# Seeding PSUM banks from ScalarE and VectorE in a seven-product matmul scheme, with a new order of the products

## The chip, the cores and the metric

The kernel runs on one core of one Trainium2 chip. The metric is device time in microseconds, the median of the runs; lower is better.

## The reference

```python
x = A_x                                   # (1, 1, 8192, 448)
xn = _layernorm(x, axis=-1)
s = _A_ref(xn, ...)                       # spectral mixer: rfft2, two block-diagonal
                                          # complex layers (4 blocks of 112), soft threshold, irfft2
g = _silu(_B_ref(xn, w_gate, w_up, w_down))
                                          # (gelu(x @ w_gate) * (x @ w_up)) @ w_down, 448 -> 1792 -> 448
return x + s * g
```

Everything is fp32. 8192 tokens go through both branches.

## The kernel before

**Precision.** Each fp32 factor is split into a high and a low fp16 part; a product of two such factors is three matmuls (high·high, low·high, high·low) that accumulate in fp32 in PSUM.

**Stages.** The FFN branch is the bulk of the work on TensorE. Its 1792 hidden columns are worked in two passes: pass p = 0 takes 8 blocks of 128 columns, pass p = 1 takes 6 (`PF`, L30). In each pass the 8192 tokens go by in 16 chunks (`NG`) of 512 tokens. The first two chunks of pass 0 are done plainly (`plain`). All others, 14 chunks of pass 0 and 16 of pass 1, use a seven-product (Strassen-Winograd) scheme over 2x2 blocks: two hidden blocks, gate and up, and two token halves. Beside the FFN run, in this order, the normalisation and forward transform (beside pass 0), the spectral groups (beside pass 1), and the inverse transform with the final gating (beside the end of pass 1).

**A unit** (`unit`, L1026) is one pair of hidden blocks of one chunk: 4 units in a chunk of pass 0, 3 in a chunk of pass 1, 104 in all. It has seven products, 1, 5, 6, 7, 2, 3 and 4 (`PROD`, `product`, L985). Products 1, 5, 6 and 7 are 12 matmuls of 256 columns, products 2, 3 and 4 are 10. Each goes into a PSUM bank of 512 fp32 columns; `start=True` on the first matmul of a group begins a sum afresh, later ones accumulate.

There are four rings of two PSUM banks each: `BX`, `BY`, `BD`, `BF` (L404). In a unit:

- X (a BX bank) takes product 1, then 6, 7 and 4 on top. ACT copies X after product 1 to `p1` (ring U1, trace name u) and after product 6 to `v1` (ring V1, trace name v); DVE adds `p5` to X after product 7 and writes `v2` (ring V2, trace name v).
- Y (a BY bank) takes product 5, which ACT copies to `p5` (ring U5, trace name u), then product 3 on top.
- Z (a BY bank) takes product 2 alone.
- `c11` on DVE adds Z to `p1`, then ACT takes the gelu of that. `c12` adds Y to `v1` on DVE, then `glu` (L1010, a scalar_tensor_tensor) multiplies gelu, scale and that sum: the hidden values of token half 0. `c21` takes the gelu of X after product 4, and `glu` multiplies it with `v2`: half 1.
- The hidden values are split to fp16 (`h`): ACT casts, DVE or POOL subtracts. In pass 1 `sums` makes the sums that the down projection's own seven-product scheme needs, in pieces of a weight tile (trace name wt).

**Order on TensorE.** `chunk` (L1442) emits, unit after unit, products 1, 5, then product 4 of the unit before, then 6, 2, 3, 7; in the last unit of a chunk of pass 1 it is 2, 7, 3. After the last unit come its product 4 and the down projection (`down` in pass 0, `down2` in pass 1, trace tiles bd). In pass 1 the last part of `down2`, called `tail`, is kept back and run in the next chunk after its first unit's product 5. Vector work after the down projection adds into `pt`.

**What sets the order of everything else.** The program is emitted by a planner (`Pace`, L49). Tasks are generators; each instruction is issued at a planned time that follows from the planner's own costs and from when the operands are ready, and the order of issue is the order in that engine's queue. The engines then run their queues in order and wait on semaphores. Rings (`Ring`, L221) hand out buffers and PSUM banks; a task that finds none free waits until one is put back. All engine calls go through one helper, so every row of the profile has its line, L199, and rows are told apart by their tiles.

Of the kernel before, what the change touches and what calls it, by code (L numbers as in the profile page):

```python
# [11 lines left out]
F32 = mybir.dt.float32  # L12
I32 = mybir.dt.int32
AF = mybir.ActivationFunctionType
ALU = mybir.AluOpType
# [6 lines left out]
NG = 16  # L22
# [351 lines left out]
def afno_geglu_kernel(ctx, tc, x, gu, wd, mlp, b1, b2, c_m, c_mt, c_small, out):  # L374
# [22 lines left out]
    def ring(pool, shape, dt, name, bufs):  # L397
        return Ring(pace, pool, shape, dt, name, bufs)
# [84 lines left out]
    XTB = ring(fp, [128, (XW - XA) // 128, 256], F16, "xtb", 1)  # L483
    HT = ring(fp, [128, PF[0][1], 2, 512], F16, "h", 1)
    U1 = ring(fp, [128, 512], F32, "u1", 2)
    U5 = ring(fp, [128, 512], F32, "u5", 1)
    V1 = ring(fp, [128, 512], F32, "v1", 1)
    V2 = ring(fp, [128, 512], F32, "v2", 2)
    GL = ring(fp, [128, 512], F32, "gl", 1)
    TH = ring(fp, [128, D], F32, "th", 3)  # L490
# [534 lines left out]

    def unit(p, i, f0, h, xa):  # L1026

        m = {}

        def copy_of(R, name, bank_, at):  # L1030
            def go():
                t = m[name] = yield from R.get()
                S.copy(t, bank_)
                pace.set(m["e" + name])
            m["e" + name] = Event()
            return pace.spawn(go(), at)

        def a1():
            for e in range(2):
                yield ev("comb", f0 + e) if p == 0 else ev("far", f0 + e)  # L1040
            m["X"] = yield from BX.get()
            product(1, m["X"], xa, f0, True, False)
            copy_of(U1, "p1", m["X"], pace.last)

        def a5():
            m["Y"] = yield from BY.get()
            product(5, m["Y"], xa, f0, True, False)
            copy_of(U5, "p5", m["Y"], pace.last)

        def a6():  # L1050
            yield m["ep1"]
            product(6, m["X"], xa, f0, False, False)
            copy_of(V1, "v1", m["X"], pace.last)

        def a2():
            m["Z"] = yield from BY.get()
            product(2, m["Z"], EV["xtb", p, i], f0, True, True)
            m["c11"] = pace.spawn(c11(), pace.last)

        def c11():  # L1060
            u = m["p1"]
            V.tensor_tensor(u, m["Z"], u, op=ALU.add)
            BY.put(m["Z"])
            yield
            gelu(p, f0, u, u)
            yield

        def a3():
            yield m["ep5"]
            product(3, m["Y"], EV["xtb", p, i], f0, False, True)  # L1070
            pace.spawn(c12(), pace.last)

        def c12():
            yield m["ev1"]
            v = m["v1"]
            V.tensor_tensor(v, m["Y"], v, op=ALU.add)
            BY.put(m["Y"])
            yield
            yield m["c11"]
            if p == 1:  # L1080
                g0 = m["g0"] = yield from G0.get()

                def back():
                    V1.put(v)
                    U1.put(m["p1"])

                yield from glu(p, f0, m["p1"], v, 0, h, back, g0)
                done("h", p, i, f0, 0)
                return
            yield from glu(p, f0, m["p1"], v, 0, h, lambda: V1.put(v))  # L1090
            U1.put(m["p1"])
            done("h", p, i, f0, 0)

        def a7():
            yield m["ev1"]
            product(7, m["X"], xa, f0, False, False)
            m["ec22"], m["ev2"] = Event(), Event()
            pace.spawn(c22(), pace.last)

        def c22():  # L1100
            m["v2"] = yield from V2.get()
            V.tensor_tensor(m["v2"], m["X"], m["p5"], op=ALU.add)
            pace.set(m["ev2"])
            U5.put(m["p5"])
            yield
            pace.set(m["ec22"])

        def a4():
            yield m["ev2"]
            product(4, m["X"], EV["xtb", p, i], f0, False, True)  # L1110
            pace.spawn(c21(), pace.last)

        def c21():
            gl = yield from (GL if p == 0 else GL2).get()
            gelu(p, f0, gl, m["X"])
            BX.put(m["X"])
            yield
            yield m["ec22"]
            yield from glu(p, f0, gl, m["v2"], 1, h, lambda: V2.put(m["v2"]))
            if p == 1:  # L1120
                yield from sums(gl)
                return
            GL.put(gl)
            done("h", p, i, f0, 1)

        def sums(gl):


            yield ev("h", p, i, f0, 0)
            g0, x = m["g0"], gl[:, 512:768]  # L1130
# [24 lines left out]

    def plain(c, f):

# [284 lines left out]
    def chunk(p, i):  # L1442
# [14 lines left out]
        if p == 1:  # L1457
            pace.spawn(pt_loads(i))
            if state["direct"] <= i:
                pace.spawn(load_gate(i), pace.now + 10.0)  # L1460
        prev = None
        for u in range(nf // 2):
            six, last = unit(p, i, 2 * u, h, xa)
            for n, s in enumerate(six):
                if (u, n) == (0, 2) and "tail" in state:
                    yield from state.pop("tail")()
                if (u, n) == (0, 3):
                    yield ev("xt", "b", p, i)
                if n == 2 and prev:
                    yield from prev()  # L1470
                    if (p, i) == (0, NG - 1):
                        pace.spawn(far_pair(u - 1))
                    yield pe()
# [642 lines left out]
```

## Time and profile before

| what | value |
|---|---|
| median of 3 runs | 1813.92 us (1813.49 to 1814.45) |
| profiled execution, first to last instruction | 1811.1 us |
| instructions | 39096 |
| TensorE matmuls | 15709 |
| VectorE busy | 1395.7 us, 2497 instructions |
| ScalarE busy | 1059.9 us, 2015 instructions |
| GpSimd busy | 470.3 us, 550 instructions |
| HBM | 124 GB/s over the span |

The profile is of one execution, with busy time per engine; times in it are microseconds, means of one instruction nanoseconds. In a row, `out<-in` are the program's names, and a bracket at the end gives the idle time of the engine just before it and who ended it. Matmuls are pipelined and their ends are modelled.

### The profile page before, as it was taken

The page shows a single profiled execution, that of the slowest core. Times are in us where ns is not written, and L with a number is a line of the kernel's source. Part 1 is how long each engine was busy: PE and PEld are TensorE (multiplying, and loading weights), DVE is VectorE, ACT ScalarE, POOL GpSimd, SP SyncE. Part 2 cuts the span into 40 slices and gives each one's busy share as a digit, 9 for nine tenths or more (in the row PEclk, how much of TensorE's full clock was granted, in tenths as well). Part 3 has the DMA queues.
Part 4 walks back from the last instruction along what each step waited for, and adds up shares of the span by engine and source line. Part 5 has one row for each costly group of instructions (what it writes and reads, how often), then busy time and mean ns, then how long its engine had stood idle before and what let it go on. Part 6 is the DMA issues. An engine that isn't in the chain of part 4 may idle for free. (4 is left out here: it accounts for less than half of the span.)

```text
span 1811.1 us, 39096 instructions
## 1 busy us (share of the span) xinstructions
PE 1769.5 (98%) x15709; PEld 1429.6 (79%) x15709; DVE 1395.7 (77%) x2497; ACT 1059.9 (59%) x2015; POOL 470.3 (26%) x550
## 2 busy tenths in 40 slices
PE   7999999999999999999999999999999999999997
PEld 3447777767687777787887999999999998888886
DVE  7867888777865656656766888889888887888876
ACT  5746555645555444556676777777777674333343
POOL 3333432432221122100110322233223222232331
PEclk9999999999999999999999999999999999999999
DMA  6554776468655433322335624444335438999971
GB/s 217 159 151 125 201 202 193 148 196 233 168 131 162 135 111 94 94 66 75 88 126 155 163 83 119 119 109 92 94 104 119 114 80 222 296 303 304 291 234 44
DMA packets 345733, 277.03 MB, mean 153 GB/s; under 512 B 231536, under 2 KB 316784, under 8 KB 345552
## 3 DMA queue, kind: packets, MB, share of 16 engines
q1 hardware_dynamic: 345264, 273.98, 53.5%
q8 instruction: 123, 2.02, 0.5%
q10 hardware_dynamic: 288, 0.56, 0.1%
q14 instruction: 58, 0.48, 0.1%
HBM read 123.31 MB, written 102.02 MB: 124 GB/s over the span
## 5 line engine op out<-in xcount | busy, mean ns | idle before, releaser
L199 PEld LDWEIGHTS <-wt 128*128 128x128 f16 x9350 | 909.7, 98 | 173.3 <-issue 17.8
L199 PE MATMUL bx<-xta,wt 128*128 128x256 f16 (+1 forms) x3843 | 473.6, 275 | 0.3 <-ACT v L199 0.2
L199 PEld LDWEIGHTS <-h 128*128 128x128 f16 x2688 | 257.1, 98 | 131.8 <-DVE h L199 4.5
L199 PE MATMUL bd<-dw,h 128*128 128x448 f16 (+1 forms) x1920 | 345.5, 329 | 3.4 <-DVE h L199 2.8
L199 PE MATMUL by<-xtb,wt 128*128 128x256 f16 x2080 | 251.2, 272 | 0.0
L199 PE MATMUL by<-xta,wt 128*128 128x256 f16 (+1 forms) x1347 | 177.0, 281 | 4.1 <-DVE xta L199 3.1
L199 POOL TENSOR_TENSOR wt<-wt 128x256 f32<-128x256 f32 x90 | 72.1, 801 | 304.4 <-DVE wt L199 288.0
L199 PE MATMUL bx<-xtb,wt 128*128 128x256 f16 x1040 | 130.5, 272 | 1.8 <-DVE v L199 0.9
L199 DVE TENSOR_TENSOR u<-by,u 128x512 f32<-128x512 f32 x104 | 71.5, 688 | 57.3 <-PE by L199 55.7
L199 ACT COPY u<-bx 128x512 f32<-128x512 f32 x104 | 60.9, 585 | 74.4 <-PE bx L199 73.3
L199 ACT ACTIVATE u<-u,fc 128x512 f32<-128x512 f32 (+1 forms) x118 | 77.6, 668 | 41.9 <-DVE u L199 41.9
L199 PE MATMUL bd<-dw,wt 128*128 128x224 f16 (+1 forms) x816 | 96.0, 264 | 4.7 <-DVE pt L199 4.5
L199 ACT COPY v<-bx 128x512 f32<-128x512 f32 x104 | 60.8, 585 | 63.9 <-PE bx L199 63.4
L199 ACT CAST h<-wt 128x512 f16<-128x512 f32 (+1 forms) x128 | 68.8, 538 | 47.3 <-DVE wt L199 37.4
L199 DVE SCALAR_TENSOR_TENSOR pt<-bd,fb,pt 128x448 f32<-128x448 f32 x96 | 63.5, 680 | 39.1 <-PE bd L199 38.9
L199 ACT COPY u<-by 128x512 f32<-128x512 f32 x104 | 61.0, 587 | 52.5 <-PE by L199 48.6
L199 ACT ACTIVATE th<-bd,fb 128x448 f32<-128x448 f32 x62 | 39.1, 632 | 83.5 <-PE bd L199 71.6
L199 PE MATMUL bf<-w2t,wn 112*128 112x112 f16 x1512 | 84.9, 213 | 0.0
L199 DVE SCALAR_TENSOR_TENSOR gl<-v,fc,gl 128x512 f32<-128x512 f32 (+1 forms) x70 | 47.8, 699 | 45.6 <-ACT gl L199 45.4
L199 PEld LDWEIGHTS <-wn 112*128 112x128 f16 x1512 | 80.6, 98 | 2.4
L199 DVE TENSOR_TENSOR v<-by,v 128x512 f32<-128x512 f32 x104 | 71.0, 683 | 6.4 <-PE by L199 5.8
L199 PEld LDWEIGHTS <-w1t 112*112 112x112 f16 x612 | 68.6, 130 | 7.9 <-issue 3.3
(218 smaller groups left out, 3037.7 us busy)
## 6 DMA issues: line engine op xcount, KB each, us to landing
xts<-sx SPq DMA_DIRECT2D x32, 480.0 KB, 3.1
x<-in_x SPq DMA_DIRECT2D x17, 896.0 KB, 6.4
t<-ysb SPq DMA_DIRECT2D x64, 224.0 KB, 3.3
prt<-th SPq DMA_DIRECT2D x64, 224.0 KB, 2.2
pt<-prt SPq DMA_DIRECT2D x64, 224.0 KB, 3.9
u<-t SPq DMA_DIRECT2D x32, 448.0 KB, 5.7
x<-in_x SPq DMA_DIRECT2D x32, 448.0 KB, 6.2
y<-t SPq DMA_DIRECT2D x30, 448.0 KB, 4.0
```

The lines of the kernel that those rows point to most:

```text
L199: return self.pace.issue(self.name, kind, out, ins, lambda: fn(out, *args, **kw))
```

## The change

- **Seed of Z.** Product 1's copy is written by ACT into a BY bank instead of SBUF (`seed`), and product 2 accumulates onto it (`start=False`). The gelu of half 0 reads Z directly, so the add of `c11` is gone.
- **Seed of Y.** After product 6, DVE adds X and `p5` and writes the sum over Y's bank (`sum5`); product 3 accumulates onto it. The copy `v1`, its ring and the add of `c12` are gone; `glu` of half 0 reads Y from PSUM, and Y is given back after it. Products 3 and 7 wait for `sum5`.
- **Rings.** V1 goes, U5 has two buffers instead of one.
- **Order.** Product 4 of the unit before comes after product 6 instead of before it, and product 1 of the next unit is emitted between products 3 and 7.
- **One more matmul in each `down2`**, 64 columns wide: a bank of BY is used there with 448 columns only, and the matmul writes the remaining 64 without `start`, so that all 512 columns have been written by TensorE since the last `start`.

```diff
-    U5 = ring(fp, [128, 512], F32, "u5", 1)
-    V1 = ring(fp, [128, 512], F32, "v1", 1)
+    U5 = ring(fp, [128, 512], F32, "u5", 2)
...
+        def seed():
+
+            m["Z"] = yield from BY.get()
+            S.copy(m["Z"], m["X"])
+            pace.set(m["e1"])
...
         def a6():
-            yield m["ep1"]
+            yield m["e1"]
             product(6, m["X"], xa, f0, False, False)
-            copy_of(V1, "v1", m["X"], pace.last)
+            pace.spawn(sum5(), pace.last)
+
+        def sum5():
+            yield m["e5"]
+            V.tensor_tensor(m["Y"], m["X"], m["p5"], op=ALU.add)
+            pace.set(m["eu"])
 
         def a2():
-            m["Z"] = yield from BY.get()
-            product(2, m["Z"], EV["xtb", p, i], f0, True, True)
-            m["c11"] = pace.spawn(c11(), pace.last)
+            yield m["e1"]
+            product(2, m["Z"], EV["xtb", p, i], f0, False, True)
+            pace.spawn(c11(), pace.last)
 
         def c11():
-            u = m["p1"]
-            V.tensor_tensor(u, m["Z"], u, op=ALU.add)
+            u = m["u"] = yield from U1.get()
+            gelu(p, f0, u, m["Z"])
             BY.put(m["Z"])
             yield
-            gelu(p, f0, u, u)
-            yield
+            pace.set(m["e11"])
 
         def a3():
-            yield m["ep5"]
+            yield m["eu"]
             product(3, m["Y"], EV["xtb", p, i], f0, False, True)
             pace.spawn(c12(), pace.last)
 
         def c12():
-            yield m["ev1"]
-            v = m["v1"]
-            V.tensor_tensor(v, m["Y"], v, op=ALU.add)
-            BY.put(m["Y"])
-            yield
-            yield m["c11"]
+            yield m["e11"]
+            u, to = m["u"], None
             if p == 1:
...
+            def back():
+                BY.put(m["Y"])
+                if p == 1:
+                    U1.put(u)
+
+            yield from glu(p, f0, u, m["Y"], 0, h, back, to)
...
         def a7():
-            yield m["ev1"]
+            yield m["eu"]
             product(7, m["X"], xa, f0, False, False)
...
-        return [a1, a5, a6, a2, a7, a3] if p == 1 and f0 == PF[1][1] - 2 else [a1, a5, a6, a2, a3, a7], a4
+        return a1, a5, a6, a4, a2, a3, a7
...
         z = yield from BY.get()
         yield from prod2(2, i, h, z, 0, 2, first=True)
+        T.matmul(z[:, 2 * DH:], h[:, 0, 0, 0:128], dw[0][:, 0, 0:512 - 2 * DH], start=False, stop=False,
+                 skip_group_check=True)
...
+        units = [unit(p, i, f0, h, xa) for f0 in range(0, nf, 2)]
+        yield from units[0][0]()
+        yield pe()
         prev = None
-        for u in range(nf // 2):
-            six, last = unit(p, i, 2 * u, h, xa)
-            for n, s in enumerate(six):
...
+        for u, (_, a5, a6, a4, a2, a3, a7) in enumerate(units):
+            yield from a5()
+            yield pe()
+            if u == 0 and "tail" in state:
+                yield from state.pop("tail")()
+            yield from a6()
+            yield pe()
+            if u == 0:
+                yield ev("xt", "b", p, i)
+            else:
+                yield from prev()
...
+            yield from a2()
+            yield pe()
+            for s in (a3, units[u + 1][0], a7) if u + 1 < len(units) else (a7, a3) if p == 1 else (a3, a7):
                 yield from s()
                 yield pe()
-            prev = last
+            prev = a4
```

More of the change, by code (lines that the diff above doesn't have):

```diff
@@ L1026, in unit @@
     def unit(p, i, f0, h, xa):
[L1028 to L1036, printed above, removed]
+        m = {k: Event() for k in ("e1", "e5", "eu", "ev2", "e11")}
         def a1():
@@ L1042, in a1 @@
             product(1, m["X"], xa, f0, True, False)
-            copy_of(U1, "p1", m["X"], pace.last)
+            pace.spawn(seed(), pace.last)
+        def seed():
+            m["Z"] = yield from BY.get()
+            S.copy(m["Z"], m["X"])
+            pace.set(m["e1"])
         def a5():
@@ L1047, in a5, with copy5 @@
             product(5, m["Y"], xa, f0, True, False)
-            copy_of(U5, "p5", m["Y"], pace.last)
+            pace.spawn(copy5(), pace.last)
+        def copy5():
+            m["p5"] = yield from U5.get()
+            S.copy(m["p5"], m["Y"])
+            pace.set(m["e5"])
         def a6():
-            yield m["ep1"]
+            yield m["e1"]
             product(6, m["X"], xa, f0, False, False)
-            copy_of(V1, "v1", m["X"], pace.last)
+            pace.spawn(sum5(), pace.last)
[3 more added lines that the diff above has]
+            pace.set(m["eu"])
         def a2():
-            m["Z"] = yield from BY.get()
-            product(2, m["Z"], EV["xtb", p, i], f0, True, True)
-            m["c11"] = pace.spawn(c11(), pace.last)
+            yield m["e1"]
+            product(2, m["Z"], EV["xtb", p, i], f0, False, True)
+            pace.spawn(c11(), pace.last)
         def c11():
-            u = m["p1"]
-            V.tensor_tensor(u, m["Z"], u, op=ALU.add)
+            u = m["u"] = yield from U1.get()
+            gelu(p, f0, u, m["Z"])
             BY.put(m["Z"])
             yield
-            gelu(p, f0, u, u)
-            yield
+            pace.set(m["e11"])
         def a3():
-            yield m["ep5"]
+            yield m["eu"]
             product(3, m["Y"], EV["xtb", p, i], f0, False, True)
@@ L1073, in c12 @@
         def c12():
-            yield m["ev1"]
-            v = m["v1"]
-            V.tensor_tensor(v, m["Y"], v, op=ALU.add)
-            BY.put(m["Y"])
-            yield
-            yield m["c11"]
-            if p == 1:
[L1081 to L1091, printed above, removed]
+            yield m["e11"]
+            u, to = m["u"], None
+            if p == 1:
+                to = m["g0"] = yield from G0.get()
+            def back():
[3 more added lines that the diff above has]
+            yield from glu(p, f0, u, m["Y"], 0, h, back, to)
+            if p == 0:
+                U1.put(u)
             done("h", p, i, f0, 0)
         def a7():
-            yield m["ev1"]
+            yield m["eu"]
             product(7, m["X"], xa, f0, False, False)
-            m["ec22"], m["ev2"] = Event(), Event()
             pace.spawn(c22(), pace.last)
@@ L1102, in c22 @@
             V.tensor_tensor(m["v2"], m["X"], m["p5"], op=ALU.add)
+            U5.put(m["p5"])
             pace.set(m["ev2"])
-            U5.put(m["p5"])
-            yield
-            pace.set(m["ec22"])
         def a4():
@@ L1117, in c21 @@
             yield
-            yield m["ec22"]
             yield from glu(p, f0, gl, m["v2"], 1, h, lambda: V2.put(m["v2"]))
@@ L1460, in chunk @@
                 pace.spawn(load_gate(i), pace.now + 10.0)
+        units = [unit(p, i, f0, h, xa) for f0 in range(0, nf, 2)]
+        yield from units[0][0]()
+        yield pe()
         prev = None
-        for u in range(nf // 2):
-            six, last = unit(p, i, 2 * u, h, xa)
-            for n, s in enumerate(six):
[L1465 to L1473, printed above, removed]
+        for u, (_, a5, a6, a4, a2, a3, a7) in enumerate(units):
[9 more added lines that the diff above has]
+                yield from prev()
+                if (p, i) == (0, NG - 1):
+                    pace.spawn(far_pair(u - 1))
+                yield pe()
+            yield from a2()
+            yield pe()
+            for s in (a3, units[u + 1][0], a7) if u + 1 < len(units) else (a7, a3) if p == 1 else (a3, a7):
                 yield from s()
                 yield pe()
-            prev = last
+            prev = a4
         XTA.put(xa)
```

## The prediction

> **What bounds the kernel now.** I read the page's first part and the row of granted clock, then the busy time by stage, then TensorE's own waits, and last the timelines.
>
> ```profile
> span 1811.1 us, 39096 instructions
> PE 1769.5 (98%) x15709; PEld 1429.6 (79%) x15709; DVE 1395.7 (77%) x2497; ACT 1059.9 (59%) x2015; POOL 470.3 (26%) x550
> ...
> PEclk9999999999999999999999999999999999999999
> ```
>
> TensorE is busy in 98% of the span at the full granted clock. No other engine is near that: the PE row gives DVE 1395.7 us (77%) and ACT 1059.9 us (59%). The span is 2.8 us short of the median of the runs (1813.92 us, 1813.49 to 1814.45), so I make the sum on the span and add 2.8 us at the end.
>
> ```profile
> 0.00:60.00 60.00, 43.60 (x235) 22.61 (x235) 47.85 (x112) 37.67 (x82) 24.06 (x29) 0.97 0.58 200
> 60.00:755.00 695.00, 690.28 (x5056) 493.56 (x5056) 507.57 (x943) 377.86 (x672) 196.38 (x271) 1.00 0.56 158
> 755.00:1000.00 245.00, 245.00 (x2323) 195.87 (x2321) 156.81 (x295) 159.18 (x319) 18.45 (x19) 1.00 0.38 106
> 1000.00:1480.00 480.00, 476.78 (x5197) 438.77 (x5196) 420.05 (x730) 348.90 (x702) 143.68 (x141) 1.00 0.43 105
> 1480.00:1811.10 331.10, 313.85 (x2907) 278.75 (x2904) 263.43 (x420) 136.28 (x244) 87.69 (x90) 0.99 0.78 238
> 1801.79 0.74 PE L199 MATMUL bd<-wt,h 128*128 128x224 f16 x6
> ```
>
> These are the stages: start, the forward transform beside the first half of the FFN, an FFN-only stretch, the spectral stage beside the second half, and the last stretch. TensorE's idle time is window minus busy: 16.4, 4.7, 0, 3.2 and 17.3 us. The last matmul ends at 1802.5 us, so 8.6 us of the last figure is a tail of vector work and stores that this change does not touch; nor does it touch the first 60 us. What it can reach is 4.7 + 3.2 + 8.7 = 16.6 us. Who ends these waits:
>
> ```profile
> PE bd L199 <- DVE pt L199: 5.0, 13, 1.2
> PE bd L199 <- DVE h L199: 3.0, 4, 1.0
> PE bf L199 <- DVE k L199: 2.2, 7, 0.3
> PE bf L199 <- DVE dmx L199: 2.2, 1, 2.2
> PE bd L199 <- POOL h L199: 1.3, 2, 1.1
> PE bx L199 <- DVE v L199: 0.9, 3, 0.5
> PE bx L199 <- ACT v L199: 0.2, 1, 0.2
> ```
>
> Columns: total, times, longest. Two things matter for reading it. A busy TensorE here is also an efficient one, as the spacing of its matmuls shows:
>
> ```profile
> 717.59 1.47 PE L199 MATMUL bx<-xta,wt 128*128 128x256 f16 x12
> 718.90 1.47 PE L199 MATMUL by<-xta,wt 128*128 128x256 f16 x12
> ...
> 720.21 1.47 PE L199 MATMUL bx<-xta,wt 128*128 128x256 f16 x12
> ...
> 721.52 2.35 PE L199 MATMUL by<-xtb,wt 128*128 128x256 f16 x20
> ...
> 721.87 1.09 DVE L199 TENSOR_TENSOR xs<-x,xs 128x896 f16<-128x896 f32 x1 [8.70 <-ACT xs L199]
> ...
> 723.71 2.56 PE L199 MATMUL bx<-xta,wt 128*128 128x256 f16 x22
> ```
>
> Product 1 starts at 717.59, product 5 at 718.90, product 6 at 720.21, products 2 and 3 together at 721.52, product 7 at 723.71. Twelve matmuls take 1.31 us, twenty take 2.19 us: 109 ns each with nothing between. So product 1, 5, 6 or 7 occupies TensorE for 1.31 us, product 2, 3 or 4 for 1.09 us. Second, the modelled end runs past the next start: the row for product 1 is 1.47 us long, 0.16 us more than its slot. Every wait in the list is therefore about 0.16 us dearer than shown, and a wait shorter than that does not show.
>
> **The change part by part.** The products themselves stay: the same 78 matmuls in each of 104 units. What moves is the work that joins them.
>
> ```profile
> L199 DVE TENSOR_TENSOR u<-by,u 128x512 f32<-128x512 f32 x104 | 71.5, 688 | 57.3 <-PE by L199 55.7
> L199 DVE TENSOR_TENSOR v<-bx,u 128x512 f32<-128x512 f32 x104 | 71.0, 683 | 4.7 <-PE bx L199 4.2 <-ACT wt L199 0.3
> L199 DVE TENSOR_TENSOR v<-by,v 128x512 f32<-128x512 f32 x104 | 71.0, 683 | 6.4 <-PE by L199 5.8
> L199 ACT COPY v<-bx 128x512 f32<-128x512 f32 x104 | 60.8, 585 | 63.9 <-PE bx L199 63.4
> L199 ACT ACTIVATE gl<-bx,fc 128x512 f32<-128x512 f32 x42 | 28.9, 687 | 32.8 <-PE bx L199 26.4 <-DVE st L199 6.3
> L199 DVE SCALAR_TENSOR_TENSOR wt<-v,fc,u 128x512 f32<-128x512 f32 x48 | 45.5, 949 | 0.2
> L199 DVE SCALAR_TENSOR_TENSOR u<-v,fc,u 128x512 f32<-128x512 f32 x42 | 32.9, 783 | 1.6
> L199 DVE SCALAR_TENSOR_TENSOR u<-by,fc,u 128x512 f32<-128x512 f32 x16 | 11.9, 744 | 8.2 <-ACT u L199 8.2
> L199 PE MATMUL bx<-xtb,wt 128*128 128x256 f16 x1040 | 130.5, 272 | 1.8 <-DVE v L199 0.9
> ```
>
> *Removed.* The copy of product 1+6 (v<-bx): 60.8 us of ACT. The add of product 2 (u<-by,u): 71.5 us of DVE. The add of product 3 (v<-by,v) gives its place to the add that writes the Y bank, so of three adds per unit two remain. All this runs beside TensorE; the list shows 0.2 us for the copy and nothing for the two adds directly. Taken from the totals, DVE goes to about 1395.7 - 71.5 = 1324 us. Worth on the path: not 132 us but only what the waits return.
>
> *Made cheaper or dearer.* Half 0's multiply takes its `up` operand from PSUM instead of SBUF. The nearest row with that shape is the plain chunks' u<-by,fc,u, 744 ns; with both operands in SBUF the means are 949 and 783 ns. I take 744 ns. [...]
>
> *Writes into PSUM by ACT and DVE.* No row of before shows one. For ACT's seed of Z I bound it by 585 ns (the copy row) and 687 ns (the dearest 512-wide ACT row quoted); it must be done before product 6, 1.31 us after product 1 in the first unit of a chunk and 2.62 us in the others, so either end is covered. For DVE's add into Y the bounds are 683 ns, the same add into SBUF, and 949 ns, the slowest 512-wide mean; I take 683 because inputs and length are the same.
>
> *The new wait.* Product 3 now waits for that add instead of for ACT's copy of product 5. How late a vector operation comes is read near the end, where DVE is idle ahead of it:
>
> ```profile
> 1778.78 0.68 DVE L199 TENSOR_TENSOR v<-bx,u 128x512 f32<-128x512 f32 x1
> 1779.51 1.25 PE L199 MATMUL bx<-xtb,wt 128*128 128x256 f16 x10 [0.31 <-DVE v L199]
> 1781.91 1.26 PE L199 MATMUL by<-xtb,wt 128*128 128x256 f16 x10
> 1783.00 1.47 PE L199 MATMUL bx<-xta,wt 128*128 128x256 f16 x12
> 1783.20 0.69 DVE L199 TENSOR_TENSOR u<-by,u 128x512 f32<-128x512 f32 x1 [0.39 <-PE by L199]
> ```
>
> Product 2 hands over at 1783.00, the add starts at 1783.20; another add ends at 1779.46 and TensorE starts on it at 1779.51. So a free DVE needs 0.20 + 0.69 + 0.05 = 0.94 us. Between products 6 and 3 stand product 4 of the unit before and product 2, 2.18 us: covered, with room for one queued operation. In the first unit of a chunk only product 2 stands there, 1.09 us: a margin of 0.15 us. If DVE is then in another operation of 0.68 us, the wait is 0.53 us. In the 14 seven-product chunks of the first half nothing else fills the gap; between zero and 14 x 0.53 = 7.4 us. In the chunk quoted above DVE had been idle for 8.70 us until 721.87 and would take the add at 721.72; only a background operation that the planner puts first, such as the 1.09 us one there, would make it late. I take 0.5 us. With 949 ns the margin is -0.11 us, 14 x 0.11 = 1.5 us; that goes into the range. What queues behind a late add is the multiply of half 0 and the add for v2, which product 4 awaits.
>
> *Product 1 of the next unit ahead of product 7.* It claims its X bank 2.18 us after the previous unit's product 4 instead of 4.8 us (which had products 6, 2, 3 and 7 between); the gelu that frees it needs 0.20 + 0.69 = 0.89 us. It seeds Z early, and Z's old bank is freed by a gelu after product 2, 2.4 us before. Y is now held until the multiply: 0.94 us, and product 5 comes 2.62 us after product 3. All covered; for lagging queues I charge 0.3 us. No DMA is issued in the moved step, and neither SP's nor POOL's queue is passed. At a chunk's end nothing is gained in distance: products 7, 3, 4 stand as before in the second half.
>
> *Sixteen extra matmuls* of 64 columns, one per chunk of the second half, with a weight load each: between 0.109 x 64/256 = 0.027 us and 0.109 us, taken at 0.055: 0.9 us, fully on TensorE.
>
> *What the waits return.* (a) Product 4's wait on v2: the row bx<-xtb,wt shows 1.8 us of idle time in all, and with 0.16 us for ten such waits (an estimate; one of them, 0.31 us, is in the fence above) 3.4 us. At a chunk's end the add of product 2 is gone from DVE's queue ahead of v2's add, and the sum for Y stands earlier; I take 2.5. (b) The waits on h, 3.0 + 1.3 us in six, 5.3 with 0.16 each: half 0's chain loses one add of 0.68 us, 4.1 us at most in six; I take 2.5, since some wait for half 1. (c) pt: 5.0 us in 13; 13 x 0.20, the plain delay read above, stays, which leaves 2.4. I take 1.0. (d) k: 2.2 us in seven, from DVE's order in the spectral stage: 0.5. (e) dmx and the rest: nothing. Where these go, the next thing late is the pt add itself, then TensorE's own stream.
>
> Sum: -2.5 - 2.5 - 1.0 - 0.5 = -6.5; +0.5 + 0.3 + 0.9 = +1.7; together -4.8 us. Span 1806.3, time 1809.1 us.
>
> **The rivals.** *A: the add into Y comes late (slower).* DVE serves it in order, and DVE is busy 420.05 of 480 us in the spectral stage. One operation ahead of it in all 30 first units costs up to 30 x 0.53 = 15.9 us; at half of that, with 0.9 us of matmuls and only 2.5 us returned, +6.3: 1820.2. It decides once DVE is held more than 0.15 us past product 6's result. Against it: in the second half pieces of the other stages' matmuls stand between.
> *B: TensorE takes nothing back.* The path is the stream of 109 ns slots; v2 and pt are late for other vector work. Only 2 us return, 1.7 go: 1813.6.
> *C: banks.* Y and Z are held longer and BY has two: product 5 waits for the multiply. The price is DVE's lag beyond 2.62 us; three operations ahead give 0.94 + 3 x 0.68 - 2.62 = 0.36 us, in one unit of eight 4.7 us on top of the sum: 1813.8; in one of three 12.5 us, 1821.6. [...] No row of before shows TensorE waiting for a bank of the units.
> *D: nearly all goes.* (a), (b) and the excess of pt and k: 3.4 + 5.3 + 2.4 + 2.2 = 13.3 less 1.7: 1802.3.
>
> **How the numbers follow.** A measurement of this kernel tells about 0.2%, 3.6 us, from no change. Forecast 0.52: its own range is 1805 to 1812, of which 0.39 lies below 1810.3 and 0.13 above. D 0.12, faster. B 0.10, within. C 0.07: 0.03 within, 0.04 slower. A 0.19, slower. Faster 0.51, same 0.26, slower 0.23. The range leaves out half of A and the far side of D and C: 1801 to 1819.
>
> **What would show it.** ACT's busy time falls by about 61 us, DVE's by 72 to 83 (71.5, and 48 x 0.205 + 42 x 0.039 for the multiplies); v<-by,v and u<-by,u are gone, a TENSOR_TENSOR by<-bx,u stands in their place at 0.68 us. TensorE's busy time stays, its waits on v and h shrink to 3 us or less, and no wait on by at product 3 totals over 1 us. Rival A would show as PE by <- DVE by with some 30 waits; C as by<-xta waiting for the multiply. I am wrong if TensorE's matmuls are spaced wider than 109 ns, or if the planner, which re-orders every queue from its own costs, puts spectral or pt work ahead of the unit's adds.

## The result and the profile after

The changed kernel takes 1806.45 us (median of 5 runs, 1803.36 to 1807.7), beside 1814.45 us for the kernel before in the same session (1813.49 to 1815.79). The ratio is 0.9952, 95% interval 0.9939 to 0.9964: 8.0 us faster. The profiled execution went from a span of 1811.1 us to 1804.6 us, 6.5 us less. The 1.5 us between the two figures are no gain of their own: in a later session the median run of the kernel before took 1814.92 us with a span of 1812.9 us, so the profiled execution before was one of its faster ones. The forecast was 1809.1 us, 4.8 us less than before, so direction and range held and the gain was larger than forecast.

First part of the page of the changed kernel:

```profile
span 1804.6 us, 38978 instructions
PE 1769.2 (98%) x15725; PEld 1430.9 (79%) x15725; DVE 1339.9 (74%) x2441; ACT 997.5 (55%) x1911; POOL 401.6 (22%) x502
```

TensorE is as busy as before (1769.5 then), so nearly all of the 6.5 us (6.2) is idle time of TensorE that is gone. ACT lost 62.4 us of work. DVE lost 55.8, but POOL lost 68.7 without one edit that touches it: the planner chooses DVE or POOL for a part of the subtractions and sums, and it gave DVE more of them (POOL's instructions: 502 instead of 550).

Busy time by stage of the changed kernel, same columns as in the prediction (window, PE, weight loads, DVE, ACT, POOL, clock, DMA share, GB/s). The last window runs past the end, so only its busy times are read:

```profile
60.00:755.00 695.00, 691.50 (x5063) 494.30 (x5062) 484.14 (x910) 353.07 (x629) 180.73 (x261) 1.00 0.56 158
...
1000.00:1480.00 480.00, 479.61 (x5256) 443.39 (x5254) 402.35 (x715) 338.24 (x690) 129.70 (x139) 1.00 0.45 109
1480.00:1820.00 340.00, 308.95 (x2846) 274.61 (x2843) 251.26 (x409) 117.13 (x206) 58.70 (x64) 0.99 0.74 229
```

TensorE's idle time in the first stage went from 4.7 to 3.5 us, in the spectral stage from 3.2 to 0.4, and after 1480 us from 17.3 to 15.7 (1804.6 - 1480 - 308.95). The spectral stage gave most. In its inner 400 us the same view shows TensorE filled completely; the row of the kernel before first:

```profile
1050.00:1450.00 400.00, 397.25 (x4340) 366.17 (x4338) 350.59 (x609) 292.42 (x583) 116.69 (x113) 1.00 0.43 107
```

```profile
1050.00:1450.00 400.00, 400.00 (x4396) 370.18 (x4395) 335.43 (x598) 280.33 (x569) 101.26 (x109) 1.00 0.43 107
```

TensorE's waits in the changed kernel (total, times, longest). The rows left out (fx, xta, mxr, th and POOL's xs) stand nearly the same in both kernels:

```profile
PE bd L199 <- DVE pt L199: 6.0, 16, 1.2
...
PE bx L199 <- DVE v L199: 2.4, 4, 0.9
...
PE by L199 <- DVE by L199: 0.7, 1, 0.7
PE by L199 <- DVE u L199: 0.5, 1, 0.5
PE bx L199 <- ACT by L199: 0.3, 1, 0.3
PE bx L199 <- DVE by L199: 0.3, 1, 0.3
...
PE bd L199 <- DVE xs L199: 0.2, 1, 0.2
```

There is no row for h, for k or for dmx any more. The waits on pt and v, which the forecast meant to shorten, are longer than before (5.0 and 0.9). Two rows of the kernel before that the prediction did not show are gone too, and 0.2 us on xs at another bank stand in their place:

```profile
PE bf L199 <- DVE xs L199: 0.6, 1, 0.6
PE bd L199 <- ACT wst L199: 0.6, 1, 0.6
```

The groups that answer to the removed copy and adds, in the changed kernel (busy us, mean ns | idle time of the engine just before):

```profile
L199 DVE TENSOR_TENSOR by<-bx,u 128x512 f32<-128x512 f32 x104 | 72.3, 695 | 95.3 <-PE bx L199 81.5
...
L199 ACT COPY by<-bx 128x512 f32<-128x512 f32 x104 | 59.9, 576 | 35.5 <-PE bx L199 35.3
L199 DVE SCALAR_TENSOR_TENSOR wt<-by,fc,u 128x512 f32<-128x512 f32 x48 | 35.9, 747 | 11.6 <-ACT u L199 5.7 <-PE by L199 4.9 <-ACT h L199 0.7
```

### The profile page after: what moved, and what is told of

The parts are those of the page before. It is cut to its first block, busy times and chain, and to the rows that moved or that the text cites. A ratio compares the mean times of both kernels' runs of the same rounds, so it can differ in the third digit from the quotient of the medians.

```text
span 1804.6 us, 38978 instructions
## 1 busy us (share of the span) xinstructions
PE 1769.2 (98%) x15725; PEld 1430.9 (79%) x15725; DVE 1339.9 (74%) x2441; ACT 997.5 (55%) x1911; POOL 401.6 (22%) x502
## 5 line engine op out<-in xcount | busy, mean ns | idle before, releaser
L199 DVE TENSOR_TENSOR by<-bx,u 128x512 f32<-128x512 f32 x104 | 72.3, 695 | 95.3 <-PE bx L199 81.5
L199 POOL TENSOR_TENSOR wt<-wt 128x256 f32<-128x256 f32 x78 | 61.2, 785 | 355.1 <-DVE wt L199 337.5
L199 ACT ACTIVATE u<-by,fc 128x512 f32<-128x512 f32 (+1 forms) x118 | 73.6, 636 | 49.1 <-PE by L199 48.8
L199 DVE TENSOR_TENSOR v<-bx,u 128x512 f32<-128x512 f32 x104 | 71.1, 684 | 16.5 <-PE bx L199 16.1
L199 DVE SCALAR_TENSOR_TENSOR u<-by,fc,u 128x512 f32<-128x512 f32 (+1 forms) x86 | 55.5, 659 | 33.2 <-PE by L199 20.4
L199 ACT ACTIVATE gl<-bx,fc 128x512 f32<-128x512 f32 (+1 forms) x70 | 40.5, 599 | 71.0 <-PE bx L199 69.4
L199 ACT COPY by<-bx 128x512 f32<-128x512 f32 x104 | 59.9, 576 | 35.5 <-PE bx L199 35.3
L199 ACT ACTIVATE th<-pt 128x448 f32<-128x448 f32 x64 | 37.1, 580 | 72.0 <-DVE pt L199 65.4
```

The source lines that it names most:

```text
L199: return self.pace.issue(self.name, kind, out, ins, lambda: fn(out, *args, **kw))
```

## The experiments

**The theory**, formed on the first four runs (the order alone, the seeds alone, both loads put back, the kernel before planned anew). Between two products of a unit stands a vector operation that the second one awaits; call that a joint. How long TensorE works on other products in between is the distance of the joint. It follows from the slots read in the prediction, 1.31 us for products 1, 5, 6 and 7 and 1.09 us for 2, 3 and 4, and it has to cover 0.94 us for a free DVE, and more for each operation ahead in its queue. Inside a chunk, with the seeds in place (4' is product 4 of the unit before, 1' product 1 of the next):

| order of one unit | seed Z, 1 to 6 | sum in Y, 6 to 3 | v2, 7 to 4' |
|---|---|---|---|
| old: 1 5 4' 6 2 3 7 | 2.40 | **1.09** | 2.62 |
| product 4 moved: 1 5 6 4' 2 3 7 | **1.31** | 2.18 | 3.93 |
| product 1 moved: 5 4' 6 2 3 1' 7 | 3.71 | **1.09** | **1.31** |
| both: 5 6 4' 2 3 1' 7 | 2.62 | 2.18 | 2.62 |

In the first unit of a chunk no product 4 stands between products 6 and 3, so there the sum in Y has 1.09 us in every order.

The theory says that only with both moves no joint is short, and that the shorter queues of DVE and ACT then let everything else come in time. Its rivals: the freed vector time alone gives the gain; the order alone does; or the planner, which plans every queue anew after any edit, hit on a lucky plan.

**Each part alone.** The order without the seeds, put on the kernel before:

```diff
-        return [a1, a5, a6, a2, a7, a3] if p == 1 and f0 == PF[1][1] - 2 else [a1, a5, a6, a2, a3, a7], a4
+        return a1, a5, a6, a4, a2, a3, a7
...
+        units = [unit(p, i, f0, h, xa) for f0 in range(0, nf, 2)]
+        yield from units[0][0]()
...
+            for s in (a3, units[u + 1][0], a7) if u + 1 < len(units) else (a7, a3) if p == 1 else (a3, a7):
```

> The kernel before with the new order of the products alone (product 4 of the unit before behind product 6, product 1 of the next unit between products 3 and 7), its copies and adds as they were. Theory S (the seeds take adds off DVE and copies off ACT, and that is what TensorE's waits give back): no gain, 1812 to 1817 us, waits on h and k as before. Theory O (the order, and the queues that the planner lays out anew for it, bring the gain): 1805 to 1809 us, waits on k near 0.

And the seeds with the old order, on the changed kernel (the same lines, turned round):

```diff
-        return a1, a5, a6, a4, a2, a3, a7
+        return [a1, a5, a6, a2, a7, a3] if p == 1 and f0 == PF[1][1] - 2 else [a1, a5, a6, a2, a3, a7], a4
...
+                if n == 2 and prev:
+                    yield from prev()
```

> Both seeds and the extra matmul, with the old order of the products. Theory S: 1805 to 1809 us, waits on h and k gone, VectorE busy about 1340 us. Theory O: 1813 to 1816 us. If both parts are needed, it lies between, near 1810.

The order alone took 1824.2 us, ratio 1.0052 (1.0040 to 1.0064). The seeds alone took 1814.09 us, ratio 0.9995 (0.9986 to 1.0003). Neither part gains anything, and the two together gain 8.0 us: they need each other. Waits of TensorE with the order alone:

```profile
PE bd L199 <- DVE pt L199: 9.4, 15, 1.9
PE bd L199 <- POOL h L199: 3.6, 2, 2.5
PE bf L199 <- DVE k L199: 3.1, 5, 1.2
PE bx L199 <- ACT u L199: 3.0, 3, 2.7
```

The last row is a new one. In its longest wait, 2.65 us, product 6 of a chunk's first unit waited for the copy of product 1, which stood on ACT behind casts and copies of the stage beside it; one of them had itself waited 0.85 us for DVE. That the copy needs one of two U1 buffers may have put it late in the plan, but no run shows it. The other rows are DVE's and POOL's backlog. With the seeds alone:

```profile
PE by L199 <- DVE by L199: 4.5, 11, 1.2
...
PE bx L199 <- ACT by L199: 2.2, 2, 1.6
```

Eleven waits on the sum in Y, against one in the changed kernel: the joint of 1.09 us in the table. The timeline shows one of them, again with the seeds alone:

```profile
751.86 1.25 PE L199 MATMUL by<-xtb,wt 128*128 128x256 f16 x10
...
752.89 0.75 DVE L199 SCALAR_TENSOR_TENSOR gl<-v,fc,gl 128x512 f32<-128x512 f32 x1
...
753.55 0.69 DVE L199 TENSOR_TENSOR by<-bx,u 128x512 f32<-128x512 f32 x1
...
754.30 0.92 PE L199 MATMUL by<-xtb,wt 128*128 128x256 f16 x7 [1.19 <-DVE by L199]
```

Product 6 was through at 751.86, when product 2 took over. DVE was in small spectral operations and then in the multiply of half 1, began the sum at 753.55, and TensorE stood idle for 1.19 us before product 3.

**One move at a time.** Seeds kept; first only product 4 moved, then only product 1:

```diff
-        for u, (_, a5, a6, a4, a2, a3, a7) in enumerate(units):
+        for u, (a1, a5, a6, a4, a2, a3, a7) in enumerate(units):
+            yield from a1()
+            yield pe()
...
-            for s in (a3, units[u + 1][0], a7) if u + 1 < len(units) else (a7, a3) if p == 1 else (a3, a7):
+            for s in (a7, a3) if p == 1 and u + 1 == len(units) else (a3, a7):
```

> Both seeds; of the order only product 4 moved behind product 6, product 1 left at the head of its unit. Theory T (the seeds alone gain nothing because the add into Y has only 1.09 us before product 3 in every unit, and product 4 in between gives it 2.18): waits of by on DVE by fall from 4.5 us to about 1, and the time to 1807 to 1810 us. Rival U (product 1 ahead of 7 is what counts, since it gives ACT's seed of Z 2.62 us before product 6): near 1814, waits of by on by as in the seeds-only kernel.

```diff
-            yield from a6()
-            yield pe()
-            if u == 0:
-                yield ev("xt", "b", p, i)
-            else:
+            if u > 0:
                 yield from prev()
...
+            yield from a6()
+            yield pe()
+            if u == 0:
+                yield ev("xt", "b", p, i)
```

> Both seeds; of the order only product 1 moved ahead of product 7, product 4 left ahead of product 6, so the add into Y has 1.09 us before product 3. Theory T: waits of by on DVE by near 4.5 us, 1812 to 1815 us. Rival U: 1806 to 1809 us.

Only product 4 moved: 1818.05 us, ratio 1.0015 (1.0006 to 1.0024). Only product 1 moved: 1829.68 us, ratio 1.0082 (1.0068 to 1.0096). One row of the waits with product 4 moved, and two with product 1 moved:

```profile
PE bx L199 <- ACT by L199: 5.0, 6, 1.1
```

```profile
PE bx L199 <- DVE v L199: 10.8, 15, 2.5
...
PE by L199 <- DVE by L199: 4.7, 11, 2.0
```

The largest waits between products fall on the joints set in bold in the table: the seed of Z in the first, v2 and the sum in Y in the second. With product 4 moved there are also 3.5 us in three waits on the sum in Y; 2.5 of them are one wait in the first unit of a chunk, where only product 2 stands between. These are half-steps of the change, with all its vector time saved, and they are slower than the kernel before by 2.8 and 14.5 us (1815.21 us in that session). Each was run with one plan only, so what part of these figures is the plan's is not shown.

**One seed at a time**, both in the new order. With the Y seed alone product 1 is copied to SBUF again, and DVE adds it to Z; with the Z seed alone product 6's copy and DVE's add after product 3 are back, and so is the single U5 buffer:

```diff
-            m["Z"] = yield from BY.get()
-            S.copy(m["Z"], m["X"])
+            m["u"] = yield from U1.get()
+            S.copy(m["u"], m["X"])
...
+            V.tensor_tensor(u, m["Z"], u, op=ALU.add)
```

> The changed kernel with its new order, but only the Y bank is seeded: ACT copies product 1 into a U1 buffer instead of into Z, product 2 starts Z, and DVE adds the copy to Z (the sixteen 64-column matmuls are left out). DVE gets 104 adds of 0.69 us = 72 us back. Theory (freed vector time and joints together): most of the gain goes, 1815 to 1825, DVE busy about 1410, and a wait on ACT u at product 6, since product 1's copy must wait for one of two U1 buffers. Rival (one joint alone holds the gain, and it is Y's): 1805 to 1809.

```diff
-            yield m["e5"]
-            V.tensor_tensor(m["Y"], m["X"], m["p5"], op=ALU.add)
+            m["v1"] = yield from V1.get()
+            S.copy(m["v1"], m["X"])
...
+            V.tensor_tensor(v, m["Y"], v, op=ALU.add)
```

> The changed kernel with its new order, but only the Z bank is seeded: ACT copies product 1+6 to a buffer as before the change, product 3 waits for ACT's copy of product 5 alone, and DVE adds the buffer to Y after it. DVE keeps its 104 adds for half 0 (about 72 us more than the changed kernel would not be right: one add to Y replaces one into Y, and the other add, for v2, stays; so DVE gains the add after product 3 and loses the add into Y, 0 us), ACT gets 60 us of copies back. Theory (DVE's time counts, ACT's does not, and no joint is short): 1805 to 1811. Rival (both seeds are needed): 1814 to 1820.

The Y seed alone took 1819.22 us, ratio 1.0026 (1.0017 to 1.0035), with DVE at 1381.3 us and 2.6 us of waits on ACT's u: inside the theory's range, though DVE stayed below the 1410 us expected. Its largest new waits, 5.2 us in four, are on the sum in Y. The Z seed alone took 1823.88 us, ratio 1.0056 (1.0043 to 1.0069), where the theory said 1805 to 1811 and its rival 1814 to 1820: a miss for both. Its waits:

```profile
PE bd L199 <- DVE pt L199: 8.6, 19, 2.5
...
PE bf L199 <- DVE k L199: 4.9, 8, 0.8
PE bd L199 <- POOL h L199: 2.7, 2, 2.5
```

The joints between products are not later there than in the changed kernel (3.0 us in nine waits on v); it is the work after the units, 16.2 us in these three rows against 6.0 in the changed kernel. DVE is 11.0 us busier (1350.9 us), and ACT has 50.9 us more. So the theory had left ACT out too early, and the next runs put load back on one engine at a time.

**Load put back.** To the changed kernel, three additions whose results nobody reads: ACT copies product 5 once more and DVE adds it to Z; DVE alone does one more add per unit, behind the add for v2; ACT alone does one more copy per unit at the same place (its edit is shown against that of the DVE load).

```diff
             S.copy(m["p5"], m["Y"])
+            S.copy(m["p5"], m["Y"])
...
             gelu(p, f0, u, m["Z"])
+            V.tensor_tensor(m["Z"], m["Z"], m["p5"], op=ALU.add)
```

> The changed kernel with the removed load put back in places where nothing new waits for much: ACT copies Y to p5 a second time, and after the gelu DVE adds p5 to Z in place, a value that nobody reads. Busy time rises by about 61 us on ACT and 72 us on DVE. Theory L (the gain is freed engine time): back to 1812 to 1815 us. Theory C (the gain is the shorter chain from product to hidden values, whatever the load): 1805 to 1808 us.

```diff
             V.tensor_tensor(m["v2"], m["X"], m["p5"], op=ALU.add)
-            U5.put(m["p5"])
             pace.set(m["ev2"])
+            V.tensor_tensor(m["p5"], m["v2"], m["p5"], op=ALU.add)
+            U5.put(m["p5"])
```

> The changed kernel with one more DVE add of 512 columns in each unit, behind the add of v2, into p5's buffer, which has a second one beside it; nobody reads it. VectorE busy time rises by 72 us at most. Theory L (the gain rests on the DVE time that the seeds free): 1812 to 1820 us, with waits on by, u or v grown by several us. Theory C (the shorter chains alone): 1805 to 1809 us.

```diff
-            V.tensor_tensor(m["p5"], m["v2"], m["p5"], op=ALU.add)
+            S.copy(m["p5"], m["v2"])
```

> The changed kernel with one extra ACT copy per unit that nobody reads (v2 into p5, behind the add for v2: 104 x about 0.58 us = 60 us of ACT's time), at the same place as the extra DVE add of the earlier run that cost 18 us over the changed kernel. Theory 1 (any vector time put back costs, ACT's too, since the planner deals the work that either engine can do between them): 1815 to 1825, with DVE or POOL busier than in the changed kernel. Theory 2 (only DVE's own time costs; the run with the Z seed alone was slow for the longer chain of half 0): 1804 to 1811, ACT busy about 1057, DVE about 1340.

| load put back | time, us | ratio to before (95%) | over the changed kernel | DVE, ACT, POOL busy, us |
|---|---|---|---|---|
| ACT and DVE | 1824.35 | 1.0052 (1.0040 to 1.0064) | 17.9 | 1362.2, 1051.5, 508.1 |
| DVE | 1824.12 | 1.0052 (1.0039 to 1.0064) | 17.7 | 1410.4, 994.8, 471.7 |
| ACT | 1813.91 | 0.9997 (0.9988 to 1.0006) | 7.5 | 1335.7, 1045.6, 428.1 |

The first of the three is not a load alone: its add holds Z's bank longer, and its copy stands ahead of the sum in Y. Product 5 waits 5.3 us in four for a bank there, against 0.5 in the changed kernel. In the other two runs that wait is 0.9 and 0.4 us. About 72 us of DVE work, off the path and awaited by no product, cost 17.7 us, more than twice the change's whole gain; some 60 us of ACT work cost 7.5 us, between the ranges of the two theories of that run. (The kernel before itself stood 0.5 to 0.8 us higher in these sessions.) So both engines count, DVE more. (With both loads the planner moved work on to POOL, which is why DVE shows only 22 us more.) Where the DVE load is paid:

```profile
PE bd L199 <- DVE pt L199: 9.5, 25, 1.6
PE bf L199 <- DVE dmx L199: 3.6, 1, 3.6
PE by L199 <- DVE by L199: 3.5, 7, 1.1
```

These are the waits on DVE's background work, back at once, and some on the sum in Y; k adds 2.7 us in nine. The ACT load is paid in the joints instead, 4.2 us on the seed of Z in four waits. The longest of them:

```profile
218.33 0.63 ACT L199 ACTIVATE th<-bd,fb 128x448 f32<-128x448 f32 x1 [6.39 <-DMA prt<-th]
218.86 1.14 ACT L199 ACTIVATE wo<-cb,fc 128x1024 f16<-128x1024 f32 x1
219.90 0.59 ACT L199 COPY by<-bx 128x512 f32<-128x512 f32 x1
...
220.54 0.71 PE L199 MATMUL bx<-xta,wt 128*128 128x256 f16 x5 [2.11 <-ACT by L199]
```

ACT stood idle for 6.39 us in front of an operation that waited for a store, with the seed queued behind it. A plan needs room for such a wait ahead of a seed, too: here product 6 then waited 2.11 us for it. Another 3.7 us in three waits are on the sum in Y; 2.8 of them are one wait, behind 4.5 us of DVE's background operations. These two longest waits, 2.1 and 2.8 us, and some 1.7 us of slower matmuls after the first (last section) make up nearly all of the 7.5 us, so this price is not a rate per microsecond of load.

**The plan's luck.** One constant of the planner, the due time of the second stage, moved by 3 us in both kernels; the operations stay the same:

```diff
-    END1, END2, END3 = T1 + NG * DT + 12.0, 1440.0, 1770.0
+    END1, END2, END3 = T1 + NG * DT + 12.0, 1437.0, 1770.0
```

> The kernel before with one constant of its plan moved: the spectral groups are paced to a planned end at 1437 instead of 1440 us (0.7% closer together). Nothing is computed otherwise. Theory P (any new plan shifts the small waits by several us, and the change is one such draw): off by 3 us or more from 1814.5, waits on k changed. Rival: within 2 us of 1814.5, waits on k at 2 us in total as before.

> The changed kernel with the planner's constant END2 at 1437 instead of 1440, which makes it plan anew with the same operations. Theory (the gain belongs to the change, not to one lucky plan): 1804 to 1809. Rival (the plan's luck): above 1811.

The kernel before took 1814.8 us, ratio 0.9995 (0.9986 to 1.0004). The changed kernel took 1807.85 us, ratio 0.9965 (0.9952 to 0.9977). Its waits on k came back, 2.4 us in four, and the gain was still 7 us. A new plan of this kind moved the time by 0.4 and 1.4 us, which speaks against a lucky plan as the source of the 8 us. It is one small shift of each kernel; how much a plan can do after a larger edit was not measured.

**A step further.** At the end of a chunk of pass 1 products 7, 3 and 4 still follow one another, with only 1.09 us between 7 and 4. Here product 4 is put behind two thirds of the down projection's first product:

```diff
-        yield from last()
...
         yield from prod2(1, i, h, x, 0, 2, first=True)
+        yield from last()
```

> The changed kernel with the last unit's product 4 in the second half put behind the first 12 matmuls of the down projection, 1.15 us later. The waits of product 4 on v2 at a chunk's end after 1480 us (0.31, 0.31, 0.63, 0.70 and 0.26 us lost) go: 1.5 to 2.2 us less, 1804 to 1805 us, if the hidden values of half 1 aren't needed sooner. Rival: they are, the waits move to h or hs, 1806 us or more.

This took 1804.41 us (1804 to 1805 expected), ratio to before 0.9939 (0.9926 to 0.9951), the fastest of all. Its interval overlaps the changed kernel's (0.9939 to 0.9964), so that it beats the kernel before is shown, and that it beats the changed kernel is likely only. Its waits on v and pt fell to:

```profile
PE bd L199 <- DVE pt L199: 5.3, 14, 1.9
...
PE bx L199 <- DVE v L199: 1.9, 3, 0.9
```

What remains of v stands elsewhere, inside chunks. The last such wait, as the changed kernel shows it:

```profile
1728.02 1.58 DVE L199 TENSOR_TENSOR g<-g,x 128x448 f32<-128x448 f32 x1
...
1729.53 0.68 DVE L199 TENSOR_TENSOR wt<-wt,wt 128x512 f16<-128x512 f32 x1
...
1730.13 0.68 DVE L199 TENSOR_TENSOR v<-bx,u 128x512 f32<-128x512 f32 x1
...
1730.86 0.81 PE L199 MATMUL bx<-xtb,wt 128*128 128x256 f16 x6 [0.53 <-DVE v L199]
```

One long operation of the final gating and one sum for the down projection stand ahead of v2's add, and 2.62 us are not enough for the three.

**What the expectations missed.** Six of the twelve runs came out slower than every range written down for them: the order alone, product 4 alone, product 1 alone, the Z seed alone, both loads and the DVE load. The joints named some of the places of the waits; they did not give the size of the loss.

## Why the prediction was right, and where its sum was not

The forecast's frame held: TensorE's stream stays, and only its waits can return. The working against the traces, in visible waits:

| term of the forecast | forecast, us | before, us | after, us | change, us |
|---|---|---|---|---|
| (a) waits on v2 (before: 0.2 of it on the copy v1) | -2.5 | 1.1 in 4 | 2.4 in 4 | +1.3 |
| (b) waits on h | -2.5 | 4.3 in 6 | none | -4.3 |
| (c) pt | -1.0 | 5.0 in 13 | 6.0 in 16 | +1.0 |
| (d) k | -0.5 | 2.2 in 7 | none | -2.2 |
| (e) dmx, xs, wst | 0 | 3.4 in 3 | 0.2 in 1 | -3.2 |
| late sum in Y, banks, queues | +0.8 | none | 1.8 in 4 | +1.8 |
| the prediction's 0.16 us for each wait | in the terms | 33 waits | 25 waits | -1.3 |
| sixteen extra matmuls | +0.9 | | | +0.46 |
| sum | -4.8 | | | -6.44 |

The sum of the measured terms meets the span's 6.5 us. The time came out 2.7 us below the forecast's 1809.1: 1.7 us of that are in the span, and the rest is the step from span to time, taken at 2.8 us and 1.9 in the result (1806.45 - 1804.6).

**The step that failed** is the list of what the waits return. Two of its five terms, (a) and (c), had the wrong sign, and (b), (d) and (e) were too small. Term (a) was also too large to begin with: the list of waits has 0.9 us in three for it. Right was that waits return; that the sum came close is luck, since (a) and (c) missed by 5.8 us one way and (b), (d) and (e) by 6.7 the other. The prediction reasoned from the unit outward: fewer operations in the unit, so product 4 and pt come sooner. The runs show two other things. First, the order sets the distance of each joint, and the prediction priced the reordering as something merely to be covered, at 0.3 us. In the experiments the same seeds gain nothing in the old order and lose 2.8 or 14.5 us with one of the two moves. Second, what came back came at work that no product of a unit awaits: h, k, dmx and the small rows, 9.7 us, where the prediction had taken 3.0. What came back at k hangs on the plan: with the due time moved, 2.4 us of it stand again in the changed kernel. In the kernel before, k is the last of four operations that DVE runs back to back (pt, z, t, k):

```profile
1099.92 0.68 DVE L199 SCALAR_TENSOR_TENSOR pt<-bd,fb,pt 128x448 f32<-128x448 f32 x1
...
1101.45 0.42 DVE L199 TENSOR_TENSOR k<-bf,k 112x256 f32<-112x256 f32 x1
...
1101.92 0.49 PE L199 MATMUL bf<-z,w1t 112*112 112x256 f16 x3 [0.31 <-DVE k L199]
```

In the changed kernel k is done at 1077.25 and its matmuls start at 1077.86, as soon as product 5 is through, with no wait:

```profile
1076.55 1.47 PE L199 MATMUL by<-xta,wt 128*128 128x256 f16 x12
...
1076.84 0.41 DVE L199 TENSOR_TENSOR k<-bf,k 112x256 f32<-112x256 f32 x1
...
1077.86 0.49 PE L199 MATMUL bf<-z,w1t 112*112 112x256 f16 x3
```

**The prices.** DVE's write into PSUM took 695 ns (taken 683, bounds 683 and 949). ACT's took 576, just under the lower bound of 585. The multiply with its operand in PSUM took 747 ns where 744 was taken. The operand's place by itself changed little: before, half of the 48 multiplies of pass 1 from SBUF took 744 ns or less, and in the changed kernel half of the 48 with an operand in PSUM took 750 or less. The prediction read the SBUF form's mean, 949 ns, which comes from a few long ones (up to 1645 ns; see the last section); its saving of 0.2 us each came, but not because a read from PSUM is faster. An extra 64-column matmul was taken at 0.055 us. In the changed kernel the next matmul starts 28 or 29 ns behind each, 0.46 us for the sixteen.

**The rivals.** A, the late add into Y, was priced at 1820.2 us. In the changed kernel it appears once, at the very place named, the first unit of a chunk, where only product 2 stands between:

```profile
386.08 1.08 DVE L199 TENSOR_TENSOR wo<-cb,wo 128x896 f16<-128x896 f32 x1
387.08 0.69 DVE L199 TENSOR_TENSOR by<-bx,u 128x512 f32<-128x512 f32 x1
...
387.82 0.93 PE L199 MATMUL by<-xtb,wt 128*128 128x256 f16 x7 [0.72 <-DVE by L199]
```

One background operation of 1.08 us ahead gave 0.72 us. With the old order the same joint is short in every unit, and there A is real: 4.5 us in eleven waits. C, banks held longer, appears once as well, as product 5 waiting 0.5 us for the multiply (the row on u). B, nothing returned, and D, nearly all, are out by the result.

**What would show it.** ACT fell by 62.4 (61 forecast). DVE fell by 55.8 instead of 72 to 83, since it took work over from POOL, which the prediction did not foresee. Waits on h vanished; waits on v are under 3 us, yet grew; the wait on by at product 3 stayed under 1 us.

**What stays open.** Why the Z seed alone costs 17 us over the changed kernel is only partly settled. Its extra 50.9 us of ACT time would be worth about 8 us by the run with the ACT load (7.5 us for 48.1), if that were a rate. In its profiled execution two waits of 2.45 us each have a stretch at half the granted clock beside them, worth 1.5 and 1.7 us. Here is the second: product 1 takes 2.36 us instead of 1.47, and the row of the stretch (columns as in the first section) shows a clock of 0.50.

```profile
1717.41 0.73 PE L199 MATMUL bd<-dw,wt 128*128 128x224 f16 x6 [2.45 <-DVE pt L199]
...
1719.91 2.36 PE L199 MATMUL bx<-xta,wt 128*128 128x256 f16 x12
```

```profile
1718.30:1721.71 3.41, 3.41 (x20) 2.52 (x18) 3.23 (x4) 0.60 (x2) 1.47 (x1) 0.50 0.97 293
```

For the rest there is an argument, half 0's longer chain through one more add and a multiply from SBUF (867 ns in the mean where the changed kernel has 747); it was not tried by itself.

## What to carry to other kernels

In a tight TensorE stream, write down for every vector operation between two products how long TensorE works on something else, for the old order, the new one and each half-step: in this kernel the saving in vector work showed only with both seeds and in the order in which none is short inside a chunk. DVE, busy 77% of the span in the kernel before, was not free here (about 72 us of adds put back cost 17.7 us), even though no wait named its cheap operations; to price a saving on such an engine, put the same load back in a place that nobody awaits and measure it. What the saving returns may come at waits far from the edit, so look for the queue's last operation in each stage rather than at the operation that was removed.

## What the runs showed of the hardware that was not expected

ACT's copy from PSUM to PSUM was not dearer than the one to SBUF: 576 ns against 585 for the same copy in the kernel before.

The multiply of half 0 kept nearly the same duration where one operand came from PSUM: in the mean for the 48 of pass 1, 747 ns in the changed kernel, 746 with the seeds alone, 743 with both loads, 745 with the Y seed alone and 748 with the ACT load. With both operands in SBUF its mean was 949 ns in the kernel before and 867 with the Z seed alone. When the SBUF form is long stands in the traces. Of the 180 multiplies of 128x512 with both operands in SBUF in the kernel before, 27 took over 800 ns, and each of the 27 ran beside an instruction on POOL; of the 135 that ran beside none, the longest took 753 ns. In the changed kernel 36 of the 48 with an operand in PSUM ran beside POOL, and the longest took 752 ns. So beside POOL some multiplies from SBUF were long and none with an operand in PSUM was; that POOL's work is the cause is not shown, since no run changes it alone.

Some long waits of TensorE came with a cost beyond their idle time. Between 100 and 1800 us the granted clock fell to half for 3.41 us eleven times in the profiles, each time beside a wait of 1.97 to 3.60 us: twice with the order alone, with product 1 moved and with the Z seed alone, once each with product 4 moved, the Y seed alone and the three loads. Matmuls of 256 columns then started 213 ns apart instead of 109, and each stretch cost 1.3 to 1.7 us. Five other waits of 1.99 to 2.79 us had no such stretch beside them. The kernels before and after, the seeds alone, the two kernels planned anew and the step further had none there, which is part of why the slower runs are slower than their visible waits say.
